# Second gate of a two-layer mixture-of-experts kernel: weights in four column groups, rows moving, and one product that adds and turns

## The chip, the core and the metric

The kernel runs on one core of a Trainium2 chip. Its time is the device time of one execution in microseconds (us). Five engines work side by side, each through its own queue in order: TensorE (PE, the matrix array; its weight loads are listed as PEld), VectorE (DVE), ScalarE (ACT), GpSimd (POOL) and SyncE (SP), which issues most DMAs.

## What is computed

Attention with a window of 64 feeds a first mixture-of-experts layer (all 8 experts, weighted), whose output feeds a second one that sends each row to one expert. Cut to what matters here:

```python
x = attention(q, k, v)                       # 2304 rows of 512
P = sinkhorn(exp(x @ w_gate))                # first gate, 8 experts
out = sum(P[:, e] * (relu(x @ w1[e]) @ w2[e]) for e in range(8))
logits = out @ moe2_w_gate                   # second gate: 512 x 8, in fp32
# every row goes to one expert, the largest logits first, 288 rows per expert
out2[mask_e] = relu(out[mask_e] @ w1_2[e]) @ w2_2[e]
```

The second gate's logits decide by their order which expert a row goes to, and so they are made in fp32.

## The kernel before

The 2304 rows are 18 tiles of 128 rows, three tiles to a block, six blocks. `acc[:, i]` (128 rows x 512, fp32) is the first layer's output of tile i, added to for each expert in turn. For the last expert (e = 7) layer 1 of a block (`layer1s`, line 851, products of six matmuls each, line 862) and layer 2 of a tile (`layer2`, line 931, 24 matmuls at line 940) fill the array, and VectorE adds a tile's layer 2 to `acc` (line 956). After that sum the tile is final.

The order of this part is written out by hand. `layer2` calls `bg.tick()` after each third matmul and once after the tile; `stream` (line 911) puts layer-1 products and pieces of layer 2 side by side and calls `bg.tick(1, 2.3)` after some of the products. A background task is a generator; what it yields is the number of ticks until its next step. A tick of level 1 advances only tasks of level 1. Three tasks matter here:

- `held_gate` (level 1, line 1010) runs the second gate for tiles 12 to 17, whose `acc` holds seven of eight experts by then, during the layer-1 stream of blocks 0 and 1. The part of the last expert is added from its hidden units later (`held_logits`).
- `finish_all` (level 0, line 970) runs the second gate for tiles 0 to 11 once they are final, and then `to_rows`, which writes the tile as rows for the second layer: ScalarE squares the tile and sums (line 995, into `tmp[:, 1]`), VectorE makes a scale of the sum (`norm_pow2`, lines 312 to 317), ScalarE writes two scaled copies (lines 1002 and 1003), and GpSimd subtracts (line 1005), and SyncE stores (line 1006).
- `held_weights` (line 1016) is 64 VectorE sums (line 1025) that come with the ticks of layer 2.

A gate (`gate2`, line 978) is, before: four transposes of `acc[:, i]` by the identity into a PSUM tile (line 983), a copy on ScalarE into `tmp[:, 0]` (line 984), and three ticks later four products (line 988), with the turned rows as weights (128 x 128) and 8 columns of the gate's matrix moving, added up in PSUM; VectorE copies the 128 x 8 logits out (line 989).

Before layer 1's sums are evacuated, ScalarE copies products from PSUM (`sa`, `sb`, `sc`; lines 874, 886, 895), and the array's next product of the same place waits for the copy. PSUM tiles of the gate come from the pool `psb` (four), which layer 1 uses as well.

Of the kernel before, what the change touches and what calls it, by code (L numbers as in the profile page):

```python
# [8 lines left out]
F32 = mybir.dt.float32  # L9
F16 = mybir.dt.float16  # L10
I32 = mybir.dt.int32
AF = mybir.ActivationFunctionType
OP = mybir.AluOpType
# [159 lines left out]
def body(ctx, tc, q, k, v, wg1, w11, w12, wg2, w21, w22, out):  # L173
    nc = tc.nc
    V, A, PE, G, SP = nc.vector, nc.scalar, nc.tensor, nc.gpsimd, nc.sync
# [3 lines left out]
    E = wg1.shape[1]  # L179
    F = w11.shape[2]  # L180
    NT = N // 128
    DC = DM // 128
# [13 lines left out]
    psb = pss.enter_context(tc.tile_pool(name="psb", bufs=4, space=PSUM))  # L196
# [6 lines left out]
    rc = {}  # L203
# [18 lines left out]
    ident = base.tile([128, 128], F32, name="ident")  # L222
    wgs = base.tile([128, DC, 2 * E], F16, name="wgs")
    wginv = base.tile([128, 1], F32, name="wginv")
    wg2s = base.tile([128, DC, E], F32, name="wg2s")
# [744 lines left out]
    def finish_all():  # L970
        for i in range(HELD[0]):
            while i not in finals:
                yield 1
            yield 4
            yield from gate2(i, lg2[:, i])
            yield from to_rows(i)

    def gate2(i, dst):

        xT = rc["tmp"][:, 0]  # L980
        pt = psb.tile([128, 512], F32, name="pb")
        for c in range(DC):
            PE.transpose(pt[:, c * 128:(c + 1) * 128], acc[:, i, c * 128:(c + 1) * 128], ident)
        A.activation(xT, pt, AF.Copy)
        yield 3
        pl = psb.tile([128, 512], F32, name="pb")
        for c in range(DC):
            PE.matmul(pl[:, 0:E], xT[:, c * 128:(c + 1) * 128], wg2s[:, c], start=(c == 0), stop=(c == DC - 1))
        V.tensor_copy(dst, pl[:, 0:E])

    def to_rows(i, x=1):

        xs = rc["tmp"][:, x]
        m = small.tile([128, 1], F32, name="x2m")
        A.activation(xs, acc[:, i], AF.Square, accum_out=m)
        s = small.tile([128, 1], F32, name="x2s")
        inv = small.tile([128, 1], F32, name="x2inv")
        norm_pow2(m, s, inv)
        xr = st2k()[:, 0:XW]
        V.memset(xr[:, 2 * DM:], 0.0)  # L1000
        V.tensor_copy(xr[:, 2 * DM:2 * DM + 2].bitcast(F32), inv)
        A.activation(xr[:, 0:DM], acc[:, i], AF.Copy, scale=s)
        A.activation(xs, acc[:, i], AF.Copy, scale=s)  # L1003
        yield 1
        G.tensor_tensor(xr[:, DM:2 * DM], xs, xr[:, 0:DM], OP.subtract)  # L1005
        SP.dma_start(xrows[i * 128:(i + 1) * 128, :], xr)

    def held_gate():  # L1010
        for i in HELD:
            yield from gate2(i, lgh[:, i - HELD[0]])
            yield 2
        bg.done.add("lgh")
# [507 lines left out]
    for e in range(1, E):  # L1522
        bg.until(("w1", e))
        if e == 1:
            bg.until(("T", 1))
        if e == E - 1:
            bg.start("lgh", held_gate(), 1)
        run(e, [0, 1])
        bg.until(("w2", e), "gates")
        scales(e)  # L1530
        if e == E - 1:
            bg.start("finish", finish_all())
            bg.start("w2h", held_weights())
        pend[0] = [layer2(e, 0), 0]
        for b in range(2, NB):
            if e == 1:
                bg.until(("T", b))
            run(e, [b])
        bg.done.add(("l1", e))
        if e < E - 1:  # L1540
            drain(pend[0])
            pend[0] = [layer2(e, NB - 1), 0]
            drain(pend[0], 3)
            bg.done.add(("l2", e))
# [43 lines left out]
```

## Time and profile before

| what | value |
|---|---|
| three runs, median (lowest to highest) | 1925.43 us (1922.45 to 1926.74) |
| the profiled execution's own time | 1916.18 us |
| its span in the profile | 1914.4 us |
| TensorE, busy share of the span | 96% |
| VectorE, ScalarE, GpSimd | 65%, 46%, 6% |
| TensorE's granted clock, mean | 0.987 |
| the gates' products (line 988): passes, span of their starts | 144, 1405.0 to 1577.5 us |
| the gates' transposes (line 983) | 72, 1401.7 to 1574.7 us |

The profile is one execution; its durations are read from there, and the median of the runs is 9.2 us above it. A line of the timeline gives start, duration, engine, line of the kernel, operation, what is written and read, the tile of the array (rows*columns) for the array's instructions, shape and type, how many instructions of the kind follow one another, and in brackets idle time of the engine ahead of it and what ended it.

### The profile page before, as it was taken

What the parts mean: (1) busy time and instruction counts of PE and PEld (TensorE: products, weight loads), DVE (VectorE), ACT (ScalarE), POOL (GpSimd) and SP (SyncE); (2) the same over time, 40 slices, a digit from 0 to 9 for tenths busy, and PEclk for the clock granted to TensorE, in tenths of its full rate; (3) what the DMA queues carried; (4) which work ended last, traced back from release to release, by engine and by line L of the source; (5) the groups of instructions that cost most, each with busy time, mean ns of one, the idle gap of its engine ahead of it and who ended that gap; (6) DMA issues with size and microseconds to landing.
All of it is one profiled execution on the core that took longest, in us unless ns stands there. A gap on an engine that the chain in (4) does not pass through costs nothing.

```text
span 1914.4 us, 40759 instructions
## 1 busy us (share of the span) xinstructions
PE 1845.1 (96%) x16205; PEld 1319.9 (69%) x16205; DVE 1242.6 (65%) x3808; ACT 889.8 (46%) x2439; POOL 107.7 (6%) x140
## 2 busy tenths in 40 slices
PE   6999999999999999999999999999999998999987
PEld 5877555777676676767766867677677774667765
DVE  7777956664666666676667666766757767565540
ACT  6666334543455545555554555455534442222222
POOL 0000000000000000000000000000000102323231
PEclk8999999999999999999999999999999999899999
DMA  8573022320324225234351343234231111535451
GB/s 191 111 156 75 1 89 72 105 89 1 111 80 164 89 95 167 93 109 127 118 165 67 122 136 130 94 101 159 89 105 27 36 29 62 185 121 177 163 210 30
DMA packets 172799, 203.40 MB, mean 106 GB/s; under 512 B 83000, under 2 KB 130104, under 8 KB 168512
## 3 DMA queue, kind: packets, MB, share of 16 engines
q1 hardware_dynamic: 164928, 157.78, 27.1%
q0 software_dynamic: 7680, 43.02, 6.4%
q8 instruction: 127, 2.08, 0.4%
q14 instruction: 64, 0.52, 0.1%
HBM read 143.05 MB, written 57.71 MB: 105 GB/s over the span
## 4 chain that ended last, share of the span: by engine, by line
PE 74%; DVE 9%; DMA 7%; issue 5%; ACT 3%; POOL 1%; SPq 0%; POOLq 0%; ACTq 0%; DVEq 0%
PE p L940 27%; PE p L862 17%; PE pb L862 12%; PE p L770 4%; PE p L1299 4%; DMA ws<-st2k 2%; DMA raw<-in_moe_w_dram 2%; DVE st2k L347 1%; DMA raw<-xrows,idx 1%; PE pb L630 1%; DMA w2scr<-st2k 1%; PE pb L1149 1%; PE p L1311 1%; ACT st2k L345 1%; PE pb L617 1%
## 5 line engine op out<-in xcount | busy, mean ns | idle before, releaser
L940 PE MATMUL p<-w2b,hh 128*128 128x512 f16 x2304 | 686.1, 379 | 0.0
L940 PE MATMUL p<-w2b,hl 128*128 128x512 f16 x1152 | 436.6, 379 | 0.0
L940 PEld LDWEIGHTS <-hh 128*128 128x128 f16 x2304 | 221.6, 99 | 218.2 <-issue 0.7
L862 PEld LDWEIGHTS <-w1b 128*128 128x128 f16 x4032 | 340.3, 98 | 22.9 <-issue 4.2
L862 PEld LDWEIGHTS <-w1x 128*128 128x128 f16 x3024 | 256.2, 98 | 19.7 <-issue 5.9
L862 PE MATMUL p<-th,w1x 128*128 128x192 f16 x1344 | 221.3, 246 | 3.1 <-ACT sa L874 2.4
L862 PE MATMUL pb<-xh,w1b 128*128 128x192 f16 x1344 | 221.3, 246 | 0.0
L940 PEld LDWEIGHTS <-hl 128*128 128x128 f16 x1152 | 112.6, 98 | 135.4 <-issue 0.5
L862 PE MATMUL pb<-xl,w1b 128*128 128x192 f16 x672 | 165.3, 246 | 0.0
L862 PE MATMUL p<-tl,w1x 128*128 128x192 f16 x672 | 165.3, 246 | 0.0
L347 DVE SCALAR_TENSOR_TENSOR st2k<-raw,wsc,st2k 128x512 f16<-128x512 f32 x128 | 92.1, 748 | 49.9 <-ACT st2k L345 49.6
L956 DVE SCALAR_TENSOR_TENSOR acc<-p,SE,acc 128x512 f32<-128x512 f32 x126 | 94.0, 746 | 40.2 <-PE p L940 39.9
L345 ACT ACTIVATE st2k<-raw,wsc 128x512 f16<-128x512 f32 x128 | 87.0, 714 | 69.1 <-DMA ws<-st2k 54.8
L862 PE MATMUL p<-th,w1b 128*128 128x192 f16 x672 | 110.6, 246 | 3.0 <-ACT sc L895 2.9
L743 ACT ACTIVATE hh<-sb 128x192 f16<-128x192 f32 x168 | 61.0, 363 | 112.5 <-DVE sb L906 112.5
L1005 POOL TENSOR_TENSOR st2k<-tmp,st2k 128x512 f16<-128x512 f32 x18 | 24.5, 1361 | 1575.5 <-ACT tmp L1003 1554.6
L862 PE MATMUL pb<-xh,w1x 128*128 128x192 f16 x672 | 110.6, 246 | 0.0
L862 PE MATMUL p<-xh,w1b 128*128 128x192 f16 x672 | 110.6, 246 | 0.0
L743 ACT ACTIVATE hh<-sa 128x192 f16<-128x192 f32 x168 | 60.9, 363 | 106.4 <-DVE sa L880 106.4
L295 ACT ACTIVATE st2k<-raw 128x512 f16<-128x512 f32 x116 | 72.3, 624 | 80.4 <-DMA raw<-in_moe_w_dram 52.0
L744 DVE SCALAR_TENSOR_TENSOR hl<-sa,hh 128x192 f16<-128x192 f32 x168 | 60.2, 358 | 72.1 <-ACT hh L743 72.1
L744 DVE SCALAR_TENSOR_TENSOR hl<-sb,hh 128x192 f16<-128x192 f32 x168 | 60.1, 358 | 71.7 <-ACT hh L743 71.7
(308 smaller groups left out, 3280.9 us busy)
## 6 DMA issues: line engine op xcount, KB each, us to landing
raw<-in_moe_w_dram SPq DMA_DIRECT2D x128, 512.0 KB, 5.5
ws<-st2k SPq DMA_DIRECT2D x128, 256.0 KB, 4.4
w2b<-w2scr SPq DMA_DIRECT2D x28, 512.0 KB, 6.4
w2scr<-st2k SPq DMA_DIRECT2D x48, 256.0 KB, 4.3
xrows<-st2k SPq DMA_DIRECT2D x18, 257.0 KB, 3.1
vs<-in_v_dram SPq DMA_DIRECT2D x35, 128.0 KB, 4.1
ldq<-in_q_dram SPq DMA_DIRECT2D x16, 256.0 KB, 4.5
ldk<-in_k_dram SPq DMA_DIRECT2D x16, 256.0 KB, 4.8
```

The costliest lines, as they stand in the source:

```text
L295: A.activation(junk[:, 0:512], s0, AF.Square, accum_out=mp[:, c:c + 1])
L345: A.activation(hi, src, AF.Copy, scale=sc)
L347: V.scalar_tensor_tensor(lo, src, sc, hi, op0=OP.mult, op1=OP.subtract)
L617: PE.transpose(pp[:, hp], pn[:, b, hp], ident)
L743: A.activation(hh[:, f, cols], src, AF.Relu)
L744: V.scalar_tensor_tensor(hl[:, f, cols], src, 0.0, hh[:, f, cols], op0=OP.max, op1=OP.subtract)
L770: PE.matmul(p[:, 0:w], w1v[wi][:, c, fs], x[:, c, ts], start=(n == 0), stop=(n == 3 * DC - 1))
L862: PE.matmul(bank[:, 0:HB], aq[wi][:, c, fs], xq[xi][:, c], start=(start and n == 0), stop=(n == 5), skip_group_check=True)
L940: PE.matmul(p, h[:, f, js], w2v[wi][:, f], start=(n == 0), stop=(n == 3 * FC - 1))
L956: V.scalar_tensor_tensor(acc[:, i], p, SE[:, e, i:i + 1], acc[:, i], op0=OP.mult, op1=OP.add)
L1005: G.tensor_tensor(xr[:, DM:2 * DM], xs, xr[:, 0:DM], OP.subtract)
L1299: PE.matmul(p[:, 0:CAP], wv1[f // 4][w][:, c, fs], xt[:, x * DC + c], start=(n == 0), stop=(n == 3 * DC - 1))
```

## The change

The four products swap their operands. The gate's matrix is laid out once as weights, four chunks of 128 x 32 with the 8 real columns ahead and zeros behind (`gate2_weights`); chunk c stands in column group c of the array, and the turned rows move, 128 columns. The four results lie under each other in PSUM, 4 x 32 partitions by 128 rows of the tile. ScalarE copies them to the first quarter of `tmp[:, 1]`, and one more product, with that copy as weights and a 128 x 8 matrix of ones and zeros moving, adds the four chunks and turns the result to 128 x 8. The yields change with it: `finish_all` waits 2 ticks in place of 4 ahead of the gate, the gate has one more yield of 2, and `held_gate` starts with the layout of the matrices and one tick.

```diff
             while i not in finals:
                 yield 1
-            yield 4
+            yield 2
             yield from gate2(i, lg2[:, i])
             yield from to_rows(i)
...
         A.activation(xT, pt, AF.Copy)
         yield 3
+
         pl = psb.tile([128, 512], F32, name="pb")
         for c in range(DC):
-            PE.matmul(pl[:, 0:E], xT[:, c * 128:(c + 1) * 128], wg2s[:, c], start=(c == 0), stop=(c == DC - 1))
+            PE.matmul(pl[c * 32:(c + 1) * 32, 0:128], rc["wg2p"][:, c], xT[:, c * 128:(c + 1) * 128], start=True, stop=True)
+        sT = rc["tmp"][:, 1, 0:128]
+        A.activation(sT, pl[:, 0:128], AF.Copy)
+        yield 2
+        pl = psb.tile([128, 512], F32, name="pb")
+        PE.matmul(pl[:, 0:E], sT, rc["sel"], start=True, stop=True)
         V.tensor_copy(dst, pl[:, 0:E])
+
+    def gate2_weights():
+
+        w = rc["wg2p"] = rc["pool"].tile([128, DC, 32], F32, name="wg2p")
+        V.memset(w, 0.0)
+        V.tensor_copy(w[:, :, 0:E], wg2s)
+        sel = rc["sel"] = rc["pool"].tile([128, E], F32, name="sel")
+        V.tensor_copy(sel, ident[:, 0:E])
+        for c in range(1, DC):
+            V.tensor_tensor(sel, sel, ident[:, c * 32:c * 32 + E], OP.add)
...
     def held_gate():
+        gate2_weights()
+        yield 1
         for i in HELD:
             yield from gate2(i, lgh[:, i - HELD[0]])
             yield 2
```

## Rows read from the trace of the kernel before

**Rows 1.** Busy us (and instructions) of PE, PEld, DVE, ACT, POOL; clock; DMA.

```profile
1395.00:1440.00 45.00, 44.75 (x444) 39.05 (x443) 19.82 (x60) 18.86 (x58) 0.00 (x0) 1.00 0.33 109
1480.00:1520.00 40.00, 39.09 (x309) 28.08 (x308) 30.62 (x103) 17.29 (x47) 3.97 (x3) 1.00 0.20 47
```

**Rows 2.** Timeline of the array around the products of the first held gate.

```profile
1405.04 0.38 PE L940 MATMUL p<-w2b,hl 128*128 128x512 f16 x1
1405.26 0.95 PE L988 MATMUL pb<-wg2s,tmp 128*128 128x8 f32 x8
1406.07 0.24 PE L862 MATMUL p<-th,w1x 128*128 128x192 f16 x1
...
1406.56 0.59 PE L940 MATMUL p<-w2b,hh 128*128 128x512 f16 x2
```

**Rows 3.** Timeline at tile 0: its sum and its transposes.

```profile
1446.93 0.74 DVE L956 SCALAR_TENSOR_TENSOR acc<-p,SE,acc 128x512 f32<-128x512 f32 x1
...
1449.29 0.60 PE L983 MATMUL pb<-ident,acc 128*128 128x128 f32 x4
...
1449.72 0.59 PE L940 MATMUL p<-w2b,hh 128*128 128x512 f16 x2
```

**Rows 4.** Timeline in attention: fp32 products on halves of the array.

```profile
149.97 1.09 PE L593 MATMUL pb<-kring,qT 64*64 64x128 f32 x16
150.99 0.69 PE L630 MATMUL pb<-hl,ldv 128*64 128x64 f32 x16
151.60 1.09 PE L588 MATMUL pb<-kring,qT 64*64 64x128 f32 x16
```

**Rows 5.** Timeline: a single fp32 product with 8 moving columns.

```profile
394.02 0.28 PE L302 MATMUL pb<-np,ones 128*128 128x8 f32 x2
394.16 0.59 PE L940 MATMUL p<-w2b,hh 128*128 128x512 f16 x2
```

**Rows 6.** Timeline: weight loads of the second held gate's products.

```profile
1409.20 0.97 PEld L988 LDWEIGHTS pb<-wg2s,tmp 128*128 128x128 f32 x8 [0.48 <-ACT tmp L984]
```

**Rows 7.** Timeline from tile 2's gate to tile 3's transposes.

```profile
1474.19 0.62 ACT L995 ACTIVATE tmp<-acc 128x512 f32<-128x512 f32 x1
...
1474.71 0.19 ACT L995 ACTIVATION_READ_ACCUMULATOR tmp<-acc 128x1 f32 x1
1475.44 0.95 PE L988 MATMUL pb<-wg2s,tmp 128*128 128x8 f32 x8
...
1476.43 0.17 DVE L989 COPY lg<-pb 128x8 f32<-128x8 f32 x1 [1.76 <-PE pb L988]
1476.52 0.14 DVE L312 TENSOR_SCALAR pbn<-x2m 128x1 int32<-128x1 int32 x1
...
1477.26 0.72 ACT L1002 ACTIVATE st2k<-acc,x2s 128x512 f16<-128x512 f32 x1 [2.35 <-DVE x2s L316]
...
1477.41 0.68 DVE L1025 SCALAR_TENSOR_TENSOR junk<-raw,st2k 128x512 f16<-128x512 f32 x1
1477.89 0.71 ACT L1003 ACTIVATE tmp<-acc,x2s 128x512 f32<-128x512 f32 x1
...
1478.67 1.16 POOL L1005 TENSOR_TENSOR st2k<-tmp,st2k 128x512 f16<-128x512 f32 x1 [14.71 <-ACT tmp L1003]
...
1479.12 0.93 DVE L744 SCALAR_TENSOR_TENSOR hl<-sc,hh 128x192 f16<-128x192 f32 x1
...
1479.96 0.68 DVE L1025 SCALAR_TENSOR_TENSOR junk<-raw,st2k 128x512 f16<-128x512 f32 x1
...
1482.24 0.75 DVE L956 SCALAR_TENSOR_TENSOR acc<-p,SE,acc 128x512 f32<-128x512 f32 x1
...
1483.04 0.66 PE L983 MATMUL pb<-ident,acc 128*128 128x128 f32 x4 [0.46 <-DVE acc L956]
```

**Rows 8.** Timeline at tile 4: its sum and its transposes.

```profile
1488.05 0.74 DVE L956 SCALAR_TENSOR_TENSOR acc<-p,SE,acc 128x512 f32<-128x512 f32 x1
...
1489.52 0.60 PE L983 MATMUL pb<-ident,acc 128*128 128x128 f32 x4
```

## What the change should do to the time

> **What bounds the kernel now.** I read the busy times by stretch first. From 1395 to 1440 us, where the six held tiles have their second gate, the array is busy 44.75 of 45 us, and from 1480 to 1520, where three of the other twelve have theirs, 39.09 of 40, at a granted clock of 1.00 in both; VectorE is busy 19.82 of 45 and then 30.62 of 40 [rows 1]. So each us that the array loses or gains between 1400 and 1578 us moves the end, and VectorE has room, if its work comes in time. Then I read the timeline, for two things: what a gate costs on the array, and how near the gate's transposes come to VectorE's sum for their tile (`acc`, L956), which they read.
>
> **The array's own work, per gate.** Before, the four products begin at 1405.26 and the next work at 1406.07: 0.81 us, eight passes, since each fp32 product appears twice [rows 2]. The change puts in their place four products with 32 columns of weights and 128 moving fp32 columns, again two passes each, and a fifth with 8 moving columns.
>
> A pass of 128 fp32 columns takes 0.43/4 = 0.11 us (four transposes, 1449.29 to 1449.72) [rows 3]. Whether products on different column groups run side by side is shown for halves: attention's scores (64*64, 128 columns) need 1.02 us for 16 passes, not 16 x 0.11 = 1.74, and its products with the values (128*64: all rows, two column groups, 64 columns) 0.61, not 0.87 [rows 4]. Both are eight pairs (0.87 and 0.44) and some 0.15 us for the change of shape of the tile before them. For quarters no row exists. Side by side, four cost 2 x 0.11 = 0.22; as pairs 0.44; one at a time 0.87. The nearest row is 128*64, and it overlaps as far as its columns allow, so I take 0.22. A gate changes shape twice, 2 x 0.15, hence 0.52 us (ends: 0.74, 1.17). The fifth product is like the single fp32 product with 8 columns among L940: 394.02 to 394.16, 0.14 us [rows 5].
>
> Sum per gate 0.52 + 0.14 - 0.81 = -0.15; 18 gates: **-2.7 us** (pairs +1.3, one at a time +9.0).
>
> The Trainium skill ("TensorE: Matmul & The Clock Gate", Part 3: Packing small matmuls) says that weight loads overlap running matmuls only when their row groups differ. The four products here share all rows, so by that rule they would go one at a time and the sum would hold +9.0. The value products share all rows too and still need 0.61 us, not 0.87 [rows 4]: here the trace disagrees.
>
> **The six held gates.** Their steps come with the weights stream, not with the sums. I followed the yields through the stream: between transposes and products of the second held tile, the old order puts one group of six L862, and the array's weights waited 0.48 us for the copy [rows 6]; the new puts three, 1.5 us, against the copy's 0.6, and the fifth product again stands 1.1 to 1.5 us behind the fourth. So **-0.4 us**. The gate's new constants are six small VectorE operations, about 1 us, in a stretch where it is busy 44% [rows 1]: nothing on the path (1 us if it were full).
>
> **The twelve others: the order.** Here the background steps after each third L940. Before, the transposes come after 12 L940 of the next tile and the products after 21. With `yield 2` the transposes come after 6, the four products after 15, the fifth after 21. The transposes so stand 6 x 0.216 = 1.3 us earlier on the array, and array instructions go in order: behind a transpose that waits for `acc` stand all later products. And what followed the gate before, VectorE's copy of the logits and the norm, still follows the fifth product.
>
> The second new wait: the turned rows are put into `tmp[:, 1]`, where the Square (L995) of the same tile writes. Before, that Square ran at 1474.19, ahead of the gate at 1475.44 [rows 7]; now it overwrites what the fifth product reads, so it waits for that. Behind it stand, on ScalarE, the two scaled copies L1002 and L1003 and the evacuations of layer 1; on VectorE, the norm (which needs the Square's sum), then L1025, layer 1's sums and `acc` itself; on POOL L1005, and behind that on SP the store of the row and the next row of the gate weights, which is fetched eight L1025 ahead of its use (nothing).
>
> I count from the start of the fifth product, S = 0 (0.04 to 0.05 from engine to engine), with the delays of tiles 2 and 3 [rows 7] and of the single product [rows 5]: result 0.28, Square from 0.32 to its sum 1.03 (1474.19 to 1474.71 + 0.19), norm from 1.07, first scaled copy 0.74 later at 1.81 (1476.52 to 1477.26), second at 2.44 (+0.63), what follows on ScalarE at 3.06 (+0.62: the second started 0.09 ahead of the first one's end).
> - Second tile of a block (1, 4, 7, 10). Norm 1.07, L1025 at 1.96 (1476.52 to 1477.41), `acc` 0.68 later at 2.64, 0.74 long [rows 8], +0.05: transposes at 3.43. The array gets there in 0.14 + 9 x 0.216 = 2.08. Wait 1.35 us, four times **+5.4** (without an L1025 between 0.7 each, +2.8). Before: none, `acc` ended at 1488.79, the transposes began at 1489.52 [rows 8].
> - First tile of a block (3, 6, 9). The evacuation of the last layer-1 product stands behind the scaled copies: hh at 3.06, hl behind it; and POOL's L1005 starts 0.78 after the second copy, at 3.22, and the VectorE operation that met it, such an hl, took 0.93, its follower starting 1.29 after L1005 [rows 7], so L1025 at 4.51, `acc` 5.19, 0.75 long, transposes at 5.99. The array: 0.14 + one group of six, 0.49 [rows 2], + 12 x 0.216 = 3.22. Wait 2.8 (2.1 if L1005 is missed: it held the hl for the 0.71 that they shared); before 0.46 [rows 7], as at two more tiles. Three times **+7.0** (low +4.9).
> - After the second tile's gate, layer 1 copies its third result on ScalarE at 3.06, ready some 0.4 later, at 3.46; the product that needs the place comes at 0.14 + 3 x 0.216 + 4 x 0.49 = 2.75. Wait 0.7, four times **+2.8** (low 0).
> - Tile 0: `acc` ends 1447.67, its transposes begin 1449.29 [rows 3]; 1.3 earlier still fits. Third tiles have their gate a whole layer-1 stream behind their sum: nothing.
>
> These waits come one after the other, each counted from a product that itself stands behind the wait before, so they add up. **The tail**: the last evacuation of layer 1 also ends about 1.1 us later against the array; L940 still fill it there, so 0 to 1.1, taken 0.5.
>
> **The sum.** -2.7 - 0.4 + 5.4 + 7.0 + 2.8 + 0.5 = +12.6 us on the profiled execution's 1916.2 us (1914.4 of it span), 1928.8. That execution lies 9.2 below the median of the three runs, 1925.4; the difference goes onto the median: **1938.0 us**. With all low ends +4.6, 1930.0; with pairs +16.6, 1942.0.
>
> **Rivals.**
> - *The column groups don't overlap.* For it: no row shows four. Against: two do. Pairs: 1942.0. One at a time: -2.7 becomes +9.0, 1949.7. The row with 128*64 speaks against the latter [rows 4]. The rule of the Trainium skill above speaks for it.
> - *The Square doesn't wait*, as before, and only the earlier transposes cost. Norm then at 0.41: second tiles 0.7 each (+2.8), first tiles 2.1 less 0.46 (+4.9), the third copy ready in time: +5.1, 1930.5. Against: the two places are the same bytes.
> - *Cover.* VectorE idles 1.76 us ahead of the old gate [rows 7]; were that time filled with the L1025 that now stand ahead of `acc`, the waits would shrink to the gain: about +2, 1927.
> - *Faster.* If `acc` ends within six L940 of its tile's last product, no transpose waits, also not the three that do now: -2.7 - 0.4 - 3 x 0.46 = -4.5, 1920.9. It decides at 1.3 us. Counted from twelve L940 (2.59 us) ahead of the place of its transposes, tile 0's ends after 0.97 us, with VectorE's queue short, tile 4's after 1.9 and tile 3's after 3.0 [rows 3, 7, 8].
>
> **Chances.** Forecast 0.62 (1934 to 1941), pairs 0.10, one at a time 0.05, no wait of the Square 0.10, cover 0.08, faster 0.05. A measurement of this kernel tells about 0.2%, 3.9 us, from no change: faster 0.05, same 0.08, slower 0.87. The range leaves out faster, one at a time and the lower part of cover: 1928 to 1943.
>
> **What will show it.** Right: transposes (L983) of tiles 1, 3, 4, 6, 7, 9, 10 waiting for `acc` L956, 1.3 to 2.8 us each; the Square waiting for the fifth product; array busy share near 1490 falling to some 0.88; eight column-group passes from first to last in about 0.3 us. Wrong: a gate that holds the array over 0.9 us; Squares ahead of the fifth product; a granted clock under 1.00 at these waits, which I count at nothing; waits in the held stretch.

## The result, and the profile after

The changed kernel takes **1933.58 us** (median of five runs, 1933.31 to 1937.83); the kernel before, run beside it, 1922.45 (five runs, 1917.43 to 1926.74). The medians are 11.1 us apart. The ratio of the two kernels' times, which here and below is taken over the runs and not from the two medians, is 1.0066, 95% interval 1.0042 to 1.0091, or 12.7 us: slower, on the side and inside the range that was predicted. The profiled execution of after took 1933.36 us (span 1931.5), close to its median; the one of before (1916.18) lies 6 us under the median of these five runs, so the two spans differ by more than the change is worth, and the readings below go by stretches and not by spans.

**The stretches.** Busy us (and instructions) of PE, PEld, DVE, ACT, POOL, then clock and DMA, of after:

```profile
1395.00:1440.00 45.00, 44.58 (x467) 36.40 (x466) 21.55 (x69) 20.75 (x66) 0.00 (x0) 1.00 0.34 112
1480.00:1520.00 40.00, 34.56 (x289) 23.56 (x287) 28.18 (x93) 18.54 (x49) 5.12 (x4) 1.00 0.15 34
```

Beside [rows 1] the held tiles' stretch is as full as before, and the other one has lost 4.5 us of TensorE's 40: 0.86 busy. No engine became the bound: VectorE is busy 0.70 and ScalarE 0.46 of it.

**The array's own work**, timeline of PE and PEld at the first held gate of after:

```profile
1406.66 0.38 PE L940 MATMUL p<-w2b,hl 128*128 128x512 f16 x1
1406.97 0.16 PEld L989 LDWEIGHTS pb<-tmp,wg2p 128*32 128x32 f32 x8 [0.42 <-issue]
1406.97 0.42 PE L989 MATMUL pb<-tmp,wg2p 128*32 128x128 f32 x8
...
1407.33 0.60 PE L940 MATMUL p<-w2b,hh 128*128 128x512 f16 x2
```

From one L940 to the next there are 0.67 us, of which 0.216 are the L940's own step (the time from one L940's start to the next): the four products cost some 0.46 us, both changes of the tile's shape included. The eight passes last 0.42 us from the first start to the last end. The fifth product adds 0.14 (1478.07 to 1478.21 in the timeline below). So 0.60 us a gate stand in the place of 0.81 [rows 2].

**The waits** between 1395 and 1600 us on which the chain below rests (engine, what waits <- for what: us in total, times, longest), after; the two of PE are all that PE has there:

```profile
PE pb L983 <- DVE acc L956: 12.3, 7, 2.6
ACT tmp L1011 <- PE pb L994: 9.7, 12, 1.2
DVE pbn L312 <- ACT tmp L1011: 7.1, 12, 0.6
PE p L862 <- ACT sc L895: 2.4, 5, 0.5
```

Seven transposes (L983) wait for their tile's sum; before, three did, 0.46 us each [rows 7]. All twelve Squares (L1011, before L995) wait for the fifth product (L994), and the norm (L312) waits for the Square. The array also waits five times for layer 1's third copy (L895); one of these, 0.42 us at 1439, was there before the change, four are new.

**One of the long waits**, timeline from tile 2's gate to tile 3's transposes of after, the same place as [rows 7]:

```profile
1475.91 0.43 PE L989 MATMUL pb<-tmp,wg2p 128*32 128x128 f32 x8
1476.46 0.28 ACT L991 ACTIVATE tmp<-pb 128x128 f32<-128x128 f32 x1 [1.79 <-PE pb L989]
1478.07 0.28 PE L994 MATMUL pb<-sel,tmp 128*128 128x8 f32 x2
1478.21 0.24 PE L862 MATMUL pb<-xh,w1x 128*128 128x192 f16 x1
...
1478.39 0.63 ACT L1011 ACTIVATE tmp<-acc 128x512 f32<-128x512 f32 x1 [0.83 <-PE pb L994]
1479.15 0.15 DVE L312 TENSOR_SCALAR pbn<-x2m 128x1 int32<-128x1 int32 x1 [0.59 <-ACT tmp L1011]
1479.90 0.72 ACT L1018 ACTIVATE st2k<-acc,x2s 128x512 f16<-128x512 f32 x1 [0.79 <-DVE x2s L316]
1480.53 0.71 ACT L1019 ACTIVATE tmp<-acc,x2s 128x512 f32<-128x512 f32 x1
1481.08 0.38 PE L940 MATMUL p<-w2b,hl 128*128 128x512 f16 x1
1481.14 0.35 ACT L743 ACTIVATE hh<-sb 128x192 f16<-128x192 f32 x1
1481.32 1.15 POOL L1021 TENSOR_TENSOR st2k<-tmp,st2k 128x512 f16<-128x512 f32 x1 [16.95 <-ACT tmp L1019]
1481.52 1.16 DVE L744 SCALAR_TENSOR_TENSOR hl<-sb,hh 128x192 f16<-128x192 f32 x1 [0.51 <-ACT hh L743]
1482.60 0.68 DVE L1043 SCALAR_TENSOR_TENSOR junk<-raw,st2k 128x512 f16<-128x512 f32 x1
1483.21 0.74 DVE L956 SCALAR_TENSOR_TENSOR acc<-p,SE,acc 128x512 f32<-128x512 f32 x1
1484.01 0.66 PE L983 MATMUL pb<-ident,acc 128*128 128x128 f32 x4 [2.55 <-DVE acc L956]
```

This is the chain that the prediction counted from S, the fifth product's start (here 1478.07): Square at 0.32, norm at 1.08, scaled copies at 1.83 and 2.46, POOL's L1021 at 3.25, the weights' sum L1043 (before L1025) at 4.53, `acc` at 5.14, transposes at 5.94 us. Predicted were 0.32, 1.07, 1.81, 2.44, 3.22, 4.51, 5.19 and 5.99. The step from the last L940 to the transposes is 1484.01 - 1481.08 = 2.93 us where 0.216 would do, so 2.71 are lost; before, the last L940 began at 1482.20 and the step was 0.84, so 0.62 were lost [rows 7].

Tile 4, the place of [rows 8], and the third copy after tile 1's gate, both of after:

```profile
1490.80 0.75 DVE L956 SCALAR_TENSOR_TENSOR acc<-p,SE,acc 128x512 f32<-128x512 f32 x1
1491.60 0.66 PE L983 MATMUL pb<-ident,acc 128*128 128x128 f32 x4 [1.16 <-DVE acc L956]
```

```profile
1462.64 0.25 PE L862 MATMUL pb<-xh,w1b 128*128 128x192 f16 x1
1463.03 0.31 ACT L895 ACTIVATE sc<-p 128x192 f32<-128x192 f32 x1
1463.39 0.24 PE L862 MATMUL p<-th,w1b 128*128 128x192 f16 x1 [0.51 <-ACT sc L895]
```

The four second tiles' transposes (1, 4, 7, 10) stand idle 1.14 to 1.16 us; the idle time is counted from the modelled end of an L940 that is listed with 0.38 us, so the step is 1.51 to 1.54, and 1.30 are lost. At the third copy the step is 0.75 us where L862 follow each other at 0.083: 0.67 lost. Tile 0's transposes wait for nothing, as in [rows 3].

**A measure that leaves the rest out.** Between the last VectorE sum ahead of the gates and tile 11's transposes the array runs the same products in all these kernels, gates apart: tile 11's transposes stand behind the same three L940 after the same stream of layer 1, whatever the yields. 17 of the 18 gates lie in it. The two ends, of before and then of after:

```profile
1400.14 0.75 DVE L956 SCALAR_TENSOR_TENSOR acc<-p,SE,acc 128x512 f32<-128x512 f32 x1 [4.17 <-PE p L940]
1574.47 0.27 PE L983 MATMUL pb<-ident,acc 128*128 128x128 f32 x1
```

```profile
1400.63 0.75 DVE L956 SCALAR_TENSOR_TENSOR acc<-p,SE,acc 128x512 f32<-128x512 f32 x1 [4.17 <-PE p L940]
1586.81 0.27 PE L983 MATMUL pb<-ident,acc 128*128 128x128 f32 x1
```

174.33 us before, 186.18 after: +11.85. In this execution of after some 1.5 us of that is a short fall of the clock (last section); a second profile of the same kernel, below, has 184.73, +10.40. The terms read above, with 0.4 for a wait that the held tiles lost (see the part on the prediction), give 17 x (-0.21) - 0.4 + 4 x 1.30 + 3 x (2.71 - 0.62) + 4 x 0.67 = +10.2. From here on "gate stretch" means this measure, in one profile of each kernel.

### The profile page after: what moved, and what is told of

Read it like the earlier page. It is cut to its first block, busy times and chain, and to the rows that moved or that the text cites. A ratio compares the mean times of both kernels' runs of the same rounds, so it can differ in the third digit from the quotient of the medians.

```text
span 1931.5 us, 40880 instructions
## 1 busy us (share of the span) xinstructions
PE 1843.7 (95%) x16241; PEld 1309.8 (68%) x16241; DVE 1246.0 (65%) x3814; ACT 898.5 (47%) x2457; POOL 107.8 (6%) x140
## 4 chain that ended last, share of the span: by engine, by line
PE 78%; DVE 7%; issue 6%; DMA 4%; ACT 2%; POOL 1%; SPq 1%; POOLq 0%; ACTq 0%; DVEq 0%
PE p L940 32%; PE p L862 17%; PE pb L862 12%; PE p L770 4%; PE p L1317 4%; PE pb L1167 1%; PE pb L630 1%; DMA raw<-in_moe_w_dram 1%; DMA raw<-xrows,idx 1%; PE p L1329 1%; SPq L497 1%; PE pb L617 1%; DMA w2scr<-st2k 1%; PE pb L593 1%; PE pb L588 1%
## 5 line engine op out<-in xcount | busy, mean ns | idle before, releaser
L940 PE MATMUL p<-w2b,hh 128*128 128x512 f16 x2304 | 687.0, 379 | 0.0
L940 PE MATMUL p<-w2b,hl 128*128 128x512 f16 x1152 | 436.8, 379 | 0.0
L940 PEld LDWEIGHTS <-hh 128*128 128x128 f16 x2304 | 221.1, 99 | 218.1 <-issue 3.6
L862 PEld LDWEIGHTS <-w1b 128*128 128x128 f16 x4032 | 339.6, 98 | 28.0 <-issue 8.4
L862 PEld LDWEIGHTS <-w1x 128*128 128x128 f16 x3024 | 256.3, 98 | 20.4 <-issue 6.9
L862 PE MATMUL p<-th,w1x 128*128 128x192 f16 x1344 | 221.2, 246 | 4.8 <-ACT sa L874 2.9
L862 PE MATMUL pb<-xh,w1b 128*128 128x192 f16 x1344 | 221.2, 246 | 0.0
L940 PEld LDWEIGHTS <-hl 128*128 128x128 f16 x1152 | 112.7, 98 | 135.1 <-issue 0.6
L862 PE MATMUL pb<-xl,w1b 128*128 128x192 f16 x672 | 165.3, 246 | 0.0
L862 PE MATMUL p<-tl,w1x 128*128 128x192 f16 x672 | 165.3, 246 | 0.0
L862 PE MATMUL p<-th,w1b 128*128 128x192 f16 x672 | 110.6, 246 | 5.0 <-ACT sc L895 5.0
L1021 POOL TENSOR_TENSOR st2k<-tmp,st2k 128x512 f16<-128x512 f32 x18 | 24.4, 1357 | 1580.8 <-ACT tmp L1019 1566.6
L862 PE MATMUL p<-xh,w1b 128*128 128x192 f16 x672 | 110.6, 246 | 0.0
L862 PE MATMUL pb<-xh,w1x 128*128 128x192 f16 x672 | 110.6, 246 | 0.0
```

Source lines behind the costliest of these rows:

```text
L862: PE.matmul(bank[:, 0:HB], aq[wi][:, c, fs], xq[xi][:, c], start=(start and n == 0), stop=(n == 5), skip_group_check=True)
L940: PE.matmul(p, h[:, f, js], w2v[wi][:, f], start=(n == 0), stop=(n == 3 * FC - 1))
```

## The experiments

The theory: the loss is three waits of the array, made by two things: the transposes stand 1.3 us earlier against `acc`, and the Square waits for the fifth product, which holds ScalarE, the norm, VectorE's sums and POOL back; the four column groups do run side by side. The rivals: the Square's wait is not what decides (the earlier place alone is), or the swap itself costs the array what is lost. own_place, steps_421, own_place_421 and before_early were timed together, 12 runs each, against 35 of the kernel before (median 1915.53 us); after_again and one_group (6 runs each) and own_place_511 (8 runs) together against 13 runs of it (median 1925.85). Medians can be compared only within such a batch; each ratio is to the kernel before of the same batch.

| kernel | turned sums in | ticks (finish, gate, gate) | gate stretch, us against before | median, us | ratio to before (95%) |
|---|---|---|---|---|---|
| after | `tmp[:, 1]` | 2, 3, 2 | +11.9 | 1933.58 | 1.0066 (1.0042 to 1.0091) |
| after_again | `tmp[:, 1]` | 2, 3, 2 | +10.4 | 1937.44 | 1.0065 (1.0053 to 1.0077) |
| own_place | `tmp[:, 0]` | 2, 3, 2 | +3.4 | 1919.81 | 1.0016 (1.0003 to 1.0028) |
| steps_421 | `tmp[:, 1]` | 4, 2, 1 | +1.0 | 1920.70 | 1.0025 (1.0014 to 1.0037) |
| own_place_421 | `tmp[:, 0]` | 4, 2, 1 | -3.4 | 1911.41 | 0.9973 (0.9964 to 0.9982) |
| own_place_511 | `tmp[:, 0]` | 4, 2, 1; tiles 3, 6, 9: 5, 1, 1 | -5.0 | 1921.15 | 0.9977 (0.9963 to 0.999) |
| before_early | (old gate) | 2, 3 | +4.4 | 1920.00 | 1.0022 (1.0008 to 1.0036) |
| one_group | `tmp[:, 0]` | 4, 2, 1 | +11.2 | 1936.97 | 1.0065 (1.0051 to 1.008) |

**own_place: the Square set free.** The turned sums go to the first quarter of `tmp[:, 0]`, which holds the turned rows; the four products that made the sums have read those already. Everything else is the changed kernel.

```diff
-        sT = rc["tmp"][:, 1, 0:128]
+        sT = rc["tmp"][:, 0, 0:128]
```

> The turned rows go to the first quarter of tmp[:, 0], which the four products have just read, instead of tmp[:, 1]; nothing else differs from the changed kernel. Theory (two waits, the early transposes and the Square behind the fifth product, add up): the Square runs ahead of the fifth product again, the transposes of second tiles wait some 0.7 us in place of 1.30, those of first tiles 2.1 in place of 2.7, the third copy's product no longer waits 0.5; some 6 to 7 us less than the changed kernel, so 4 to 5 us over the kernel before. Rival 1 (the early transposes alone cost it, the Square's wait lies beside other work): no difference from the changed kernel, some 11 us over the kernel before. Rival 2 (the array's own work with the column groups costs it): no difference either.

Timeline around tile 2's gate and tile 3's transposes of own_place:

```profile
1474.81 0.62 ACT L1011 ACTIVATE tmp<-acc 128x512 f32<-128x512 f32 x1
1475.42 0.28 PE L994 MATMUL pb<-sel,tmp 128*128 128x8 f32 x2
...
1479.88 0.74 DVE L956 SCALAR_TENSOR_TENSOR acc<-p,SE,acc 128x512 f32<-128x512 f32 x1
1480.67 0.66 PE L983 MATMUL pb<-ident,acc 128*128 128x128 f32 x4 [1.87 <-DVE acc L956]
```

The Square now starts 0.6 us ahead of the fifth product, not 0.3 behind its start. The first tiles' transposes stand idle 1.87 us, not 2.55, the second tiles' 0.46 to 0.47, not 1.15, and the four waits for the third copy are gone. The gate stretch is 7.0 us shorter than in after_again, the median ratio half a per cent lower. With the steps as they are, one address in a scratch buffer was worth some two thirds of the loss. What is left, +3.4, stands against the array's gain of 4.0 (17 x 0.21 and 0.4), so the order of the steps still costs some 7.

**steps_421: the old place.** The transposes go back to four ticks behind the sum, and the two later waits are shortened to 2 and 1 (the held tiles keep 3 and 2); the turned sums stay in `tmp[:, 1]`.

```diff
-            yield 2
-            yield from gate2(i, lg2[:, i])
+            yield 4
+            yield from gate2(i, lg2[:, i], 2, 1)
...
-    def gate2(i, dst):
+    def gate2(i, dst, y1=3, y2=2):
...
-        yield 3
+        yield y1
...
-        yield 2
+        yield y2
```

> The changed kernel with the steps of the twelve tiles at 4, 2 and 1 ticks instead of 2, 3 and 2: the transposes stand after 12 L940 as in the kernel before, the four products after 18, the fifth after 21; the turned rows stay in tmp[:, 1]. The held tiles keep their steps. Theory: second tiles wait under 0.3 us, first tiles 1 to 1.4 (the Square still follows the fifth product), the third copy's product 0.5; 6 to 9 us less than the changed kernel, so 1 to 4 us over the kernel before. Rival 1 (early transposes alone): equal to the kernel before less the array's 0.2 us per gate, some 3 to 4 us under it. Rival 2 (column groups): some 11 us over.

Waits of steps_421 between 1395 and 1600 us, and its transposes of tile 3:

```profile
PE pb L983 <- DVE acc L956: 3.4, 3, 1.1
PE p L862 <- ACT sc L895: 2.4, 5, 0.5
ACT tmp L1011 <- PE pb L994: 5.8, 12, 0.5
```

```profile
1484.16 0.66 PE L983 MATMUL pb<-ident,acc 128*128 128x128 f32 x4 [1.14 <-DVE acc L956]
```

No second tile waits any more; the three first tiles still do, 1.14 us, and the four waits for the third copy are unchanged: both hang on the Square, which still waits, not on where the transposes stand. The gate stretch is +1.0 us, inside the 1 to 4 expected; the median is 5.2 above the one of before and the ratio gives 4.8, more than the interval explains (1.0014 to 1.0037 is 2.7 to 7.1 us). What lies behind tile 11's transposes took 336.2 to 339.3 us in the four profiles of this batch, the longest in steps_421 and the shortest in own_place, where more transposes wait; one profile each can't say where these 2 to 4 us are, and that stays open.

**own_place_421: both.**

> Both: the turned rows in tmp[:, 0] and steps of 4, 2 and 1 ticks. Theory: only the three waits of the kernel before are left, about 0.5 us each, and the array's work is 0.2 us per gate less: 3 to 4 us under the kernel before. Rival 2 (column groups): some 11 us over. If a further wait is at work that I have not seen: between.

```profile
1475.19 0.62 ACT L1011 ACTIVATE tmp<-acc 128x512 f32<-128x512 f32 x1
1475.48 0.28 PE L994 MATMUL pb<-sel,tmp 128*128 128x8 f32 x2
...
1481.66 0.74 DVE L956 SCALAR_TENSOR_TENSOR acc<-p,SE,acc 128x512 f32<-128x512 f32 x1
1482.46 0.66 PE L983 MATMUL pb<-ident,acc 128*128 128x128 f32 x4 [0.51 <-DVE acc L956]
```

Of the waits of transposes only the three old ones are left, 0.51 us idle where [rows 7] has 0.46. The gate stretch is 3.4 us shorter than before; the terms give 17 x 0.21 = 3.6 for the array and 0.4 for the held tile's wait, less 0.2 at the three waits, 3.8. **1911.41 us, ratio 0.9973 (0.9964 to 0.9982): this version beats both kernels**, the kernel before by 5.2 us by the ratio and 4.1 between the medians. The swap does what it is for, once nothing else moves with it. The gate stretch is 4.4 shorter than that of steps_421, and 3 x (1.14 - 0.51) + 4 x 0.67 is 4.6: the Square's part at the old place.

The four kernels so form a square: address shared or own, steps early or old. The address alone is worth 7.0 us with the early steps and 4.4 with the old ones; the steps alone 9.4 with the shared place (10.4 to 1.0) and 6.8 with the own one. The two causes share some 2.6 us: at the second tiles the Square's wait loses time only when the transposes stand early.

**before_early: the move without the swap.** The kernel before, with `yield 2` for `yield 4` and nothing else.

```diff
-            yield 4
+            yield 2
```

> The kernel before with yield 2 in place of 4 and nothing else: transposes after 6 L940, the four old products after 15, and with them the copy of the logits and the norm six L940 earlier too. Theory: the transposes of second tiles wait under 0.4 us (the norm is done early, so only the sum itself counts), those of first tiles some 1.3 us more than before, 1.7 to 2; 3 to 6 us over the kernel before. Rival 1 (early transposes alone make the whole loss): 11 us or more over, as the changed kernel saves 2.7 on the array.

Its transposes of tile 3:

```profile
1484.24 0.66 PE L983 MATMUL pb<-ident,acc 128*128 128x128 f32 x4 [1.75 <-DVE acc L956]
```

The three first tiles' transposes stand idle 1.75 us (before 0.46), the second tiles' never; +4.4 us in the gate stretch, 3 x 1.3 = 3.9 of it at these waits, and +4.2 us by the ratio (1.5 to 6.9). The move alone so costs the old gate 4 us. With the swap it costs more (own_place: 4 x 0.63 at the second tiles and 3 x 1.42 at the first, 6.8); both kernels copy the logits on VectorE ahead of the norm, and with the swap that copy stands two ticks later, behind the fifth product. That this is the difference is argued from the order, not tried by itself.

**after_again: the changed kernel once more**, unchanged, to have a second profile and its time beside the next two.

> The changed kernel once more, beside the others on this chip. Theory: 10 to 13 us over the kernel before, the transposes of tiles 1, 4, 7 and 10 waiting 1.3 us and those of 3, 6 and 9 2.7 us.

1.0065 again. Its waits are the same to 0.02 us (2.55 three times; 1.14 to 1.15 four times), and its gate stretch is 10.4 us over before's, 1.5 less than in the first profile; the fall of the clock there (last section) accounts for that.

**one_group: the four products one at a time.** own_place_421 with all four products in the first column group, added up in PSUM, so that the fifth only turns 32 rows.

```diff
-            PE.matmul(pl[c * 32:(c + 1) * 32, 0:128], rc["wg2p"][:, c], xT[:, c * 128:(c + 1) * 128], start=True, stop=True)
+            PE.matmul(pl[0:32, 0:128], rc["wg2p"][:, c], xT[:, c * 128:(c + 1) * 128], start=(c == 0), stop=(c == DC - 1))
...
-        PE.matmul(pl[:, 0:E], sT, rc["sel"], start=True, stop=True)
+        PE.matmul(pl[:, 0:E], sT, ident[0:32, 0:E], start=True, stop=True)
```

> On the version with the turned rows in tmp[:, 0] and steps of 4, 2 and 1 ticks: all four products in the same column group, 32 columns of weights and 128 moving, added up in PSUM; the fifth product then has 32 rows of weights and only turns. Theory (column groups run side by side, one group goes one pass at a time): eight passes need 8 x 0.11 = 0.87 us in place of 0.22, and the fifth product changes shape too, 0.1 to 0.15 more; 0.65 to 0.8 us per gate, 12 to 14 us over the version with four groups, 8 to 10 over the kernel before. Rival (weight loads of products that share their rows never overlap, so that four groups go one at a time as well): equal to the version with four groups within 3 us.

Timeline of PE and PEld at its first held gate:

```profile
1405.31 0.38 PE L940 MATMUL p<-w2b,hl 128*128 128x512 f16 x1
1405.62 0.79 PEld L989 LDWEIGHTS pb<-tmp,wg2p 128*32 128x32 f32 x8 [0.42 <-issue]
1405.62 1.06 PE L989 MATMUL pb<-tmp,wg2p 128*32 128x128 f32 x8
...
1406.62 0.60 PE L940 MATMUL p<-w2b,hh 128*128 128x512 f16 x2
...
1407.69 0.25 PE L862 MATMUL pb<-xh,w1b 128*128 128x192 f16 x1
1407.86 0.38 PE L994 MATMUL pb<-ident,tmp 32*128 32x8 f32 x2
1408.18 0.26 PE L862 MATMUL p<-th,w1x 128*128 128x192 f16 x1
```

The same eight passes, on the same operands, take 1.06 us in one column group and 0.42 in four: 0.64 us more. Their eight weight loads take 0.79 and 0.16 us. This kernel also adds the four products up in PSUM, which the other doesn't; but its pace, some 0.11 us a pass, is that of the transposes in [rows 3], which add nothing up, so the adding is not what costs. The fifth product, now a tile of 32 rows, has a change of shape of its own: 0.32 us to the next L862 in place of 0.14, and a start 0.17 behind the L862 ahead of it, where 0.083 is the step. Together some 0.9 us; by 17 gates that is 15; the gate stretch is 14.5 longer than own_place_421's, and the median 15.8 above that of own_place_511, timed beside it. That is over the 12 to 14 expected, because the fifth product's change of shape costs 0.27 us and not 0.1 to 0.15. The 0.64 us alone are 11 us by 17 gates: the side-by-side of the four groups is worth more than the whole swap gains, and without it the old form is the better one.

**own_place_511: the last three waits.** For tiles 3, 6 and 9 the transposes come one tick later yet.

```diff
-            yield 4
-            yield from gate2(i, lg2[:, i], 2, 1)
+            yield 5 if i in (3, 6, 9) else 4
+            yield from gate2(i, lg2[:, i], 1 if i in (3, 6, 9) else 2, 1)
```

> The same version with 5, 1 and 1 ticks for tiles 3, 6 and 9, whose transposes still waited 0.67 us there: the transposes 3 L940 later, the products and the fifth product where they were. Theory: those three waits go, and the four products wait some 0.2 us for the copy: about 1 us under the version with 4, 2 and 1 everywhere, 5 to 6 under the kernel before; at the edge of what can be told.

The stretch of own_place_511 (columns as above):

```profile
1480.00:1520.00 40.00, 39.92 (x325) 26.32 (x324) 31.97 (x113) 19.46 (x53) 3.98 (x3) 1.00 0.20 47
```

No transpose waits any more, TensorE is busy 39.92 of 40 us (38.97 in own_place_421), and the gate stretch is 1.6 us shorter than own_place_421's. At tiles 3, 6 and 9 the four products start 0.42 us behind the L940 ahead of them where 0.31 is the rule: the wait for the copy, expected as 0.2 us, is 0.1. The ratio, 0.9977 (0.9963 to 0.999), can't be told from 0.9973: a difference under 0.1% is below what these runs resolve, so whether it is the better of the two stays open.

## Why the prediction was right

The direction, the mechanism and the size held; term by term:

- **The array, -2.7.** Measured -0.21 us a gate, -3.8 in all. The term that was mis-sized is the change of shape: twice 0.15 was taken from [rows 4]; the four products with it took 0.46 us, not 0.52, which leaves 0.12 for each change if the eight passes take the 0.22 counted. That quarters of the array overlap, which no row had shown, is shown by 0.42 against 1.06 us.
- **The rule of the Trainium skill** ("TensorE: Matmul & The Clock Gate", Part 3: Packing small matmuls), that weight loads overlap running matmuls only when their row groups differ, doesn't hold for column groups here: the eight loads of the four groups, all on the same rows, took 0.16 us in all, inside the 0.42 us of their passes. The rule speaks of weight loads; that the products would go one at a time was the prediction's reading of it, and one_group is what that looks like, 1.06 us.
- **The held tiles, -0.4.** From the last sum ahead of the gates to tile 0's sum: 46.79 us before (1400.14 to 1446.93), 45.08 after (1400.63 to 1445.71), so -1.71; six gates at -0.21 are -1.26, and -0.45 is left. That is the old wait for the copy [rows 6]: the products of the second held gate of before started 0.50 us behind the L862 ahead of them, those of the next ones 0.08. No new wait came there.
- **Second tiles, +5.4.** 4 x 1.30 = 5.2. **First tiles, +7.0.** 3 x (2.71 - 0.62) = 6.3: the mis-sized end is the wait of before, counted as 0.46 idle, where 0.62 were lost; the new one was counted as 2.8, and 2.71 were lost. **The third copy, +2.8.** 4 x 0.67 = 2.7. **Tile 0, nothing.** None.
- **The tail, +0.5.** Not shown. What follows tile 11's transposes took 339.9 us before and 344.7 in the first profile of after, but its length goes with the batch more than with the kernel: 336.2 to 339.3 in the four kernels of the first batch, 347.4 to 348.6 in the three of the second, about the 10.3 us that lie between the medians of the kernel before in the two. Within the second batch after_again has 348.6 and own_place_511, where no transpose waits, 347.4; in the first, profiles differ by 3 us.
- **The sum.** +12.6 predicted; +10.2 by the terms read, +10.4 in the gate stretch without the clock's fall, +11.1 between the medians, +12.7 by the ratio (0.42 to 0.91% is 8.1 to 17.5). The two errors of about 1 us each, array and first tiles, are both on the side of too slow; that the ratio meets the sum to 0.1 us is luck. The time itself, 1933.58, lies just under the 1934 to 1941 given to the forecast, though inside the whole range: the 1938.0 started from a median of 1925.4, where the five runs gave 1922.45. On that base the same sum gives 1935.1.
- **The rivals.** "The Square doesn't wait" was priced 7.5 us under the forecast; own_place, which makes it true, is 7.0 us shorter in the gate stretch, with idle times that lose 0.63 and 2.03 us where 0.7 and 2.1 were counted. "Faster" asked for `acc` within six L940 of the tile's last product; it was not met, as [rows 7, 8] said. Priced at -4.5, its outcome, that no transpose waits, was reached in own_place_511 by moving the steps: -5.0 in the gate stretch. "Cover" fell: the weights' sum still stood right ahead of `acc` (L1043 at 1482.60 above), as counted.
- **The signs named ahead.** Transposes of tiles 1, 3, 4, 6, 7, 9, 10 waiting, Squares behind the fifth product, a busy share of 0.86 where 0.88 was said, eight passes in 0.42 us where 0.3 was said, all right in kind. One that was counted at nothing came: a granted clock under 1.00 at one of these waits; it cost 1.5 us.

## What to carry to other kernels

The swap of operands alone is worth 3.4 us here (gate stretch; 4.1 between the medians); the scratch address and the yields that came with it cost 14 in the gate stretch (from -3.4 to +10.4): look at each yield and each scratch address of such a change as an edit of its own. A scratch buffer that is free by its contents is not free in its queue: whoever writes it next waits, and all that stands behind that on its engine waits with it, so take the place whose next writer comes late. And before a step that reads a sum is moved earlier on an engine that runs in order, read how long ahead the sum ends: here it had 0 to 1.6 us for a move of 1.3.

## What was not expected of the hardware

**A short fall of the clock behind one wait.** Stretches of after ahead of, in and behind it (columns as above), and the transposes in it:

```profile
1517.00:1520.80 3.80, 1.78 (x9) 0.59 (x6) 3.21 (x11) 1.59 (x3) 1.15 (x1) 1.00 0.04 15
1520.80:1524.20 3.40, 2.87 (x9) 1.61 (x10) 3.18 (x9) 0.60 (x1) 0.00 (x0) 0.51 0.78 138
1524.20:1528.00 3.80, 3.80 (x26) 1.73 (x25) 0.17 (x1) 1.00 (x3) 0.00 (x0) 0.99 0.00 0
```

```profile
1521.33 1.12 PE L983 MATMUL pb<-ident,acc 128*128 128x128 f32 x4 [2.55 <-DVE acc L956]
```

TensorE waited for tile 6's sum from 1518.78 to 1521.33. Before this wait was over its granted clock fell to half, the lower level of 1.2 GHz, and it stayed there for some 3.4 us: four transposes took 1.12 us, elsewhere 0.60 to 0.66, and L940 followed each other at 0.427, not 0.216. The same wait at tiles 3 and 9 of this execution, and at all three of after_again (there 1.00 through the same work), brought no fall, with the same order of work ahead of each. So a fall of the clock that cost 1.5 us more than the wait itself stood at one such wait in six; what decides it was not tried. Four other profiles (steps_421, own_place_421, own_place_511, before_early) show a fall of the same length near 254 us, far ahead of the gates, also behind a wait of TensorE, and five don't.

**Column groups.** Four fp32 products on four column groups that share all 128 rows lasted 0.42 us, one pass after another in one group 1.06.

**A VectorE operation that meets POOL's.** The hl of 128 x 192 that began 0.20 us behind POOL's L1021 (1481.52 in the timeline above) took 1.16 us, and ended 0.2 us after POOL did (1482.68 and 1482.47); elsewhere it takes 0.35. Its follower starts 1.28 us behind POOL's start, where 1.29 was counted from [rows 7], though the hl began at another moment there: POOL's end sets the time here, not the operation's own length. Not every VectorE operation that meets POOL is held. Two that read a PSUM tile (L896 and L880, at 1463.37 and 1463.65 of after, during POOL's 1463.20 to 1464.37) took their usual 0.36 us, and so did hl from PSUM in the kernel before (1478.84); those held, in both kernels, read their tensors from SBUF alone, as did an L1043 that met POOL at 1492.18 and took 1.52 us in place of 0.68. That this is what decides is read from these cases, not tried.
